# Moving the loads of the next head group from GpSimd to ScalarE, a quarter behind each block's exponentials

## The chip, the cores and the metric

The kernel runs on one core of one Trainium2 chip. The metric is device microseconds of one execution. Most executions of a kernel agree within 0.3%. In the profile, PE is TensorE's matmuls, PEld its weight loads, DVE is VectorE, ACT is ScalarE, POOL is GpSimd and SP is SyncE; a trailing q (ACTq, SPq, POOLq) marks an engine's instruction stream, where it issues transfers. PEclk is the TensorE clock that the throttle granted, 1.00 being full speed. An execution's time is about 2.0 us more than the span of its trace (941.21 against 939.2 us for the profiled execution of the kernel before).

## The reference, cut to what matters

```python
# x: [1, 2048, 640] bf16; 32 query heads, 32 kv heads, head size 192; only the last W = 512 keys count
xn = layernorm(x)
q  = (xn @ wq) -> 32 heads                    # wq: 640 x 6144
k, v = k_cache[:, :, Sk-512:, :], v_cache[:, :, Sk-512:, :]
s  = softmax(q k^T / sqrt(192)) v @ wo        # wo: 6144 x 640
g  = silu((sigmoid(xn w_gate) * (xn w_up)) @ w_down)
out = x + s * g
```

The part with w_gate, w_up and w_down is computed first (to about 165 us) and its gate is parked in device memory as `gB_d`. All that follows is attention, and the change is there.

## The kernel before

The 32 heads are worked in 8 groups of 2 pairs (`G = 2`, `NG = 8`), and each group in 4 blocks of 512 query rows (`NST = 4`): 32 blocks `(g, s)`. A group needs 12 loads of `wq`, 4 of `k`, 4 of `v` and 1 of `wo`. While group g is computed, `load_ahead(g + 1, s)` issues the loads of group g + 1 from GpSimd; it is called ahead of the block's matmuls, so the program's order lets GpSimd run as far ahead as buffers allow. SyncE issues the transposing transfers: `kT` (keys of the next group) and `oT` (each block's attention output, which the next block's `wo` matmuls read).

```python
def load_k(hp):                        # load_v, load_wq alike, all on nc.gpsimd
    k_sb = k_pool.tile([P, KC * PC, 2, HF], BF16, name="k_sb")      # k_pool has 2 buffers
    for i in range(2):
        nc.gpsimd.dma_start(k_sb[:, :, i, :], A_k_cache[...])       # cut

def turn_k(hp):
    kT = kt_pool.tile([P, KC * PC, P], BF16, name="kT")
    nc.sync.dma_start_transpose(kT[:], k_of[hp][:].rearrange("p k i e -> p (k i e)"))

def load_ahead(g, s):
    hps = range(g * G, (g + 1) * G)
    if s == 0:
        for hp in hps: load_k(hp)
    elif s == 1:
        for hp in hps:
            load_v(hp)
            turn_k(hp)
    elif s == 2:
        for hp in hps: load_wq(hp)
    if s == NST - 1:
        load_wo(g)

def stage_s(n, pp, c):                 # scores (L428), then the exponential (L432)
    ...
    nc.scalar.activation(E_t[n, pp][:, c, :, :], ps, AF.Exp, scale=scale_qk)

def stage_pv(n, pp, i):                # P V (L444), division, then, after the pair's second head:
    ...
        oT = oT_pool.tile([P, TQ * PC, P], BF16, name="oT")
        nc.sync.dma_start_transpose(oT[:], o_st[:].rearrange("p q d -> p (q d)"))   # L457

load_wo(0)
for u in range(G * PC // 2): stage_q(0, u)
for n, (g, s) in enumerate(blocks):
    if g + 1 < NG:
        load_ahead(g + 1, s)
    for k, (pp, c) in enumerate(todo):            # 8 score steps and exponentials
        stage_s(n, pp, c)
        if ...: stage_q(n + 1, k // 2)            # q of the next block (L412)
    for k, u in enumerate(pv):                    # 4 steps
        stage_pv(*u)
        if wo: stage_wo(*wo[k])                   # wo of the block BEFORE this one (L489): reads oT
```

Two more users of GpSimd: `load_gate` and `prep_load` fetch tiles of the gate and of x (128 rows of 640, 32 and 16 of them) for the last two groups, and in the last blocks GpSimd does the final addition of an output tile (L500).

The softmax here doesn't subtract the row's maximum and nothing guards it: scores larger than these inputs give would overflow.

## Time and profile before

| | kernel before |
|---|---|
| time, median of 3 runs | 937.3 us (936.82 to 939.11) |
| time of the execution that was profiled | 941.21 us (span 939.2) |
| TensorE busy | 923.3 us, 98% |
| period of an attention block, steady | 23.83 us |
| block 1 of 32 in the profiled execution | 27.96 us |
| loads issued by GpSimd | 232 |

From the page of the kernel before: the span; busy time, share and number of instructions of each engine; the queue of GpSimd's transfers (packets, MB, share of 16 engines' span); the shares of the chain that ended last; and the transfers of `wq` (count, KB each, median us from issue to landing).

```profile
span 939.2 us, 18233 instructions
...
PE 923.3 (98%) x7945; PEld 541.1 (58%) x8025; DVE 446.9 (48%) x636; ACT 303.8 (32%) x340; POOL 222.4 (24%) x277
...
q0 software_dynamic: 13440, 38.81, 19.5%
...
PE 95%; DMA 2%; issue 1%; POOL 1%; DVE 1%; ACT 0%; SPq 0%; DVEq 0%; ACTq 0%
...
wqp<-in_A_wq_dram POOLq DMA_DIRECT2D x96, 80.0 KB, 4.9
...
```

TensorE is the limit: 98% busy, and 95% of the chain. GpSimd's 222.4 us are mostly the issuing of transfers, and hardly any of them lie on the chain (POOL 1%). What is unusual is the 2% of the chain that lies on a DMA, `oT<-o_st`. The list of what TensorE waited for (total us, times, longest us) has it as one single wait; the one below it belongs to the start of the program:

```profile
...
PE ps_all L489 <- DMA oT<-o_st: 2.3, 1, 2.3
PE ps_all L248 <- DVE warm L243: 1.5, 1, 1.5
...
```

The timeline of TensorE in the same execution (start us, length us, what; in brackets the idle time before it and what ended it) places it in block 1, whose score matmuls start at 188.32 us:

```profile
...
201.45 0.98 PE L489 MATMUL ps_all<-wo_g,oT 128*128 128x512 bf16 x5
204.75 1.15 PE L489 MATMUL ps_all<-wo_g,oT 128*128 128x512 bf16 x6 [2.33 <-DMA oT<-o_st]
205.70 2.79 PE L444 MATMUL ps_all<-v_sb_99,E 128*128 128x193 bf16 x16
208.28 2.08 PE L489 MATMUL ps_all<-wo_g,oT 128*128 128x512 bf16 x12
210.20 1.52 PE L444 MATMUL ps_all<-v_sb_101,E 128*128 128x193 bf16 x16
...
```

After the 2.33 us stop, 16 matmuls of L444 take 2.79 us where they take 1.52 us elsewhere. The view by stretch (stretch, its length, busy us of each engine, granted clock, DMA share, GB/s) says why:

```profile
...
188.30:201.40 13.10, 13.10 (x125) 6.50 (x125) 4.82 (x6) 7.67 (x8) 2.12 (x3) 1.00 1.15 149
201.40:205.00 3.60, 1.22 (x10) 0.58 (x9) 1.14 (x2) 0.08 (x1) 0.00 (x0) 1.00 1.37 114
205.00:209.00 4.00, 4.00 (x25) 3.19 (x24) 1.20 (x3) 0.00 (x0) 2.04 (x2) 0.57 1.28 148
...
```

In the third stretch the clock granted was 0.57; a narrower stretch, 205.45 to 208.86 us, has 0.50, and the clock was full on both sides of it. Stop and slow clock together make block 1 last 27.96 us, 4.13 us over the period (2.33 us of stop and half of the 3.41 us at half clock are 4.04 us of it). The cause visible before it is a burst: by GpSimd's timeline, the `wo` of group 0 and then the whole of group 1 (22 loads) are issued between 169.74 and 190.4 us, and SyncE's stream meanwhile has the two transposes of block 0 and the two of the keys, of which the latter take 14.54 us to issue. Three lines of GpSimd's timeline, two lines of SyncE's, and the time that the 64 transfers `oT` took from issue to landing (shortest, median, longest):

```profile
...
170.57 4.06 POOL L123 DMA_DIRECT2D k_sb<-in_A_k_cache_dram  x4
...
186.03 3.57 POOL L151 DMA_DIRECT2D wqp<-in_A_wq_dram  x5 [0.54 <-DMA v_sb_111<-in_A_v_cache_dram]
189.59 0.84 POOL L379 DMA_DIRECT2D wo_g<-in_A_wo_dram  x1
...
186.95 4.02 SPq L457 DMA_TRANSPOSE oT<-o_st  x2
191.06 14.54 SPq L158 DMA_TRANSPOSE kT<-k_sb  x2
...
DMA to landing us min/median/max: 3.6/3.9/15.0
```

### The profile page before, as it was taken

The page shows a single profiled execution, that of the slowest core. Times are in us where ns is not written, and L with a number is a line of the kernel's source. Part 1 is how long each engine was busy: PE and PEld are TensorE (multiplying, and loading weights), DVE is VectorE, ACT ScalarE, POOL GpSimd, SP SyncE. Part 2 cuts the span into 40 slices and gives each one's busy share as a digit, 9 for nine tenths or more (in the row PEclk, how much of TensorE's full clock was granted, in tenths as well). Part 3 has the DMA queues.
Part 4 walks back from the last instruction along what each step waited for, and adds up shares of the span by engine and source line. Part 5 has one row for each costly group of instructions (what it writes and reads, how often), then busy time and mean ns, then how long its engine had stood idle before and what let it go on. Part 6 is the DMA issues. An engine that isn't in the chain of part 4 may idle for free.

```text
span 939.2 us, 18233 instructions
## 1 busy us (share of the span) xinstructions
PE 923.3 (98%) x7945; PEld 541.1 (58%) x8025; DVE 446.9 (48%) x636; ACT 303.8 (32%) x340; POOL 222.4 (24%) x277
## 2 busy tenths in 40 slices
PE   9999999989999999999999999999999999999996
PEld 5545445555555565555556556555566665665664
DVE  5453522434444444444444444444444444444655
ACT  4333322433333333333333333333333333333340
POOL 0060000620042004200410041004010207966005
PEclk9999999999999999999999999999999999999999
DMA  9566130692257225622664175326632543553434
GB/s 290 144 124 119 21 92 15 151 143 50 44 102 140 38 43 102 137 41 37 109 118 61 35 110 111 68 34 110 110 69 35 96 68 84 128 144 89 99 84 118
DMA packets 160383, 87.18 MB, mean 93 GB/s; under 512 B 139184, under 2 KB 151600, under 8 KB 160304
## 3 DMA queue, kind: packets, MB, share of 16 engines
q1 hardware_dynamic: 146864, 47.20, 27.2%
q0 software_dynamic: 13440, 38.81, 19.5%
q8 instruction: 63, 1.03, 0.5%
q14 instruction: 16, 0.13, 0.0%
HBM read 44.70 MB, written 5.24 MB: 53 GB/s over the span
## 4 chain that ended last, share of the span: by engine, by line
PE 95%; DMA 2%; issue 1%; POOL 1%; DVE 1%; ACT 0%; SPq 0%; DVEq 0%; ACTq 0%
PE ps_all L412 21%; PE ps_all L489 21%; PE ps_all L444 19%; PE ps_all L428 17%; PE ps_all L319 10%; PE ps_all L339 6%; DMA oT<-o_st 2%; PE ps_all L260 1%; POOL o_sb L500 1%; DMA x_sb_138<-in_A_x_dram 0%; ACT E L432 0%; DVE t_sb L499 0%; POOL gBa_sb L462 0%; DVE o_st L451 0%; DVE stats L222 0%
## 5 line engine op out<-in xcount | busy, mean ns | idle before, releaser
L432 ACT ACTIVATE E<-ps_all 128x1024 bf16<-128x1024 f32 x256 | 247.8, 1022 | 500.4 <-PE ps_all L428 453.4
L489 PE MATMUL ps_all<-wo_g,oT 128*128 128x128 bf16 (+2 forms) x1473 | 225.6, 296 | 5.6 <-DMA oT<-o_st 2.3
L417 DVE CAST qT<-ps_all 128x1024 bf16<-128x1024 f32 x96 | 117.6, 1225 | 226.3 <-PE ps_all L412 226.3
L428 PE MATMUL ps_all<-qT,kT 64*128 64x512 bf16 x1536 | 186.7, 376 | 0.0
L444 PEld LDWEIGHTS <-E 128*128 128x128 bf16 x2048 | 172.0, 98 | 24.6 <-issue 13.3
L489 PEld LDWEIGHTS <-oT 128*128 128x128 bf16 x1536 | 121.6, 98 | 78.9 <-DMA oT<-o_st 2.7
L412 PEld LDWEIGHTS <-wqp 64*128 64x128 bf16 x1920 | 93.4, 94 | 113.8 <-issue 0.3
L428 PEld LDWEIGHTS <-kT 64*128 64x128 bf16 x1536 | 72.3, 94 | 91.8 <-issue 8.4
L451 DVE TENSOR_TENSOR o_st<-ps_all,rden 128x768 bf16<-128x768 f32 x128 | 122.6, 958 | 4.9 <-DVE rden L450 0.5
L151 POOL DMA_DIRECT2D wqp<-in_A_wq_dram x96 | 68.8, 727 | 12.0 <-DMA wqp<-in_A_wq_dram 8.6
L450 DVE RECIPROCAL rden<-ps_all 128x4 f32<-128x4 f32 x128 | 23.4, 182 | 100.1 <-PE ps_all L444 99.9
L325 DVE TENSOR_TENSOR hT_sb<-ps_all,sig_sb 128x512 bf16<-128x512 f32 x48 | 33.1, 692 | 51.0 <-PE ps_all L319 41.2
L412 PE MATMUL ps_all<-xnT_95,wqp 64*128 64x512 bf16 x240 | 55.7, 376 | 0.0
L412 PE MATMUL ps_all<-xnT_96,wqp 64*128 64x512 bf16 x240 | 55.7, 376 | 0.0
L412 PE MATMUL ps_all<-xnT_94,wqp 64*128 64x512 bf16 x240 | 55.7, 376 | 0.0
L412 PE MATMUL ps_all<-xnS_91,wqp 64*128 64x512 bf16 x240 | 55.6, 376 | 0.0
L412 PE MATMUL ps_all<-xnS_92,wqp 64*128 64x512 bf16 x240 | 55.6, 376 | 0.0
L412 PE MATMUL ps_all<-xnS_90,wqp 64*128 64x512 bf16 x240 | 55.6, 376 | 0.0
L412 PE MATMUL ps_all<-xnT_93,wqp 64*128 64x512 bf16 x240 | 55.4, 376 | 0.0
L412 PE MATMUL ps_all<-xnS_89,wqp 64*128 64x512 bf16 x240 | 55.3, 376 | 0.0
L339 PE MATMUL ps_all<-wd_sb,hT_sb 128*128 128x128 bf16 (+1 forms) x377 | 52.4, 298 | 0.4
L123 POOL DMA_DIRECT2D k_sb<-in_A_k_cache_dram x32 | 32.5, 1021 | 68.2 <-DMA kT<-k_sb 68.2
(163 smaller groups left out, 742.7 us busy)
## 6 DMA issues: line engine op xcount, KB each, us to landing
wqp<-in_A_wq_dram POOLq DMA_DIRECT2D x96, 80.0 KB, 4.9
wo_g<-in_A_wo_dram POOLq DMA_DIRECT2D x8, 960.0 KB, 8.3
k_sb<-in_A_k_cache_dram POOLq DMA_DIRECT2D x32, 192.0 KB, 4.7
gBa_sb<-gB_d POOLq DMA_DIRECT2D x32, 160.0 KB, 2.7
gB_d<-gB_sb POOLq DMA_DIRECT2D x16, 160.0 KB, 2.5
xa_sb<-in_A_x_dram POOLq DMA_DIRECT2D x16, 160.0 KB, 3.2
out_dram<-o_sb SPq DMA_DIRECT2D x15, 160.0 KB, 2.3
wd_sb<-in_B_w_down_dram SPq DMA_DIRECT2D x1, 1920.0 KB, 11.8
```

Source lines behind the costliest of these rows:

```text
L123: nc.gpsimd.dma_start(k_sb[:, :, i, :], A_k_cache[0, hk, Sk - W:Sk, :].rearrange("(p k) (j e) -> p (k j) e", k=KC, j=PC),)
L151: nc.gpsimd.dma_start(wqp[r, jj // 2, :, i, :], wq_r[:, :, :, d0:d0 + HF].rearrange("p c h n -> p (c h) n"),)
L319: nc.tensor.matmul(gu[:, i, :], lhsT=w[:, c, f * P:(f + 1) * P], rhs=xnT[s][:, c, :], start=(c == 0), stop=(c == NCD - 1),)
L325: nc.vector.tensor_tensor(hT_sb[:, f, :], gu[:, 1, :], sig_sb[:], ALU.mult)
L339: nc.tensor.matmul(oB_ps[:, d0:d0 + dsz], lhsT=hT_sb[:, f, q * P:(q + 1) * P], rhs=wd_sb[:, f, d0:d0 + dsz], start=(f == 0), stop=(f == NF ...
L412: nc.tensor.matmul(ps[:, b, :], lhsT=wq_t[g][r, u, 2 * c + h].rearrange("p i e -> p (i e)"), rhs=x[s][r, c, :], start=(c == 0 and h == 0), ...
L417: nc.vector.tensor_copy(qT_t[n][:, 2 * u:2 * u + 2, :], ps)
L428: nc.tensor.matmul(ps[:, b, :], lhsT=kT[r, c * PC + j, :], rhs=qT[r, pp * PC + j, :], start=(j == 0), stop=(j == PC - 1),)
L432: nc.scalar.activation(E_t[n, pp][:, c, :, :], ps, AF.Exp, scale=scale_qk)
L444: nc.tensor.matmul(o_ps[:, q // 2, q % 2, 0:DH + 1], lhsT=E[:, c, i, q * P:(q + 1) * P], rhs=vt[:, c, 0:DH + 1], start=(c == 0), stop=(c = ...
L451: nc.vector.tensor_tensor(o_st[:, :, i * DH:(i + 1) * DH].rearrange("p (b i) d -> p b i d", b=2), o_ps[:, :, :, 0:DH], rden[:].to_broadcas ...
L489: nc.tensor.matmul(oA[:, d0 - base:d0 - base + dsz], lhsT=oT_t[n, pp][:, q * PC + j, :], rhs=wo_t[g][:, cc, d0:d0 + dsz], start=(cc == 0), ...
```

## The change

The intent is to spread the loads of the next group over its four blocks and to take their issue from GpSimd to ScalarE, placed right behind the block's eighth exponential, where ScalarE would idle for 11.6 us. Block 0 of a group issues the first pair's 6 `wq` and 2 `k` loads, block 1 the second pair's, block 2 the 4 `v` loads and the key transposes, block 3 `wo`. The loads of group 0 stay on GpSimd. The diff, cut to its core:

```diff
-    def load_k(hp):
+    def load_k(hp, eng):                      # likewise load_v, load_wq, load_wo
...
-            nc.gpsimd.dma_start(
+            eng.dma_start(
...
     def load_ahead(g, s):
-        hps = range(g * G, (g + 1) * G)
-        if s == 0:
-            for hp in hps:
-                load_k(hp)
-        elif s == 1:
-            for hp in hps:
-                load_v(hp)
+        if s < G:
+            load_wq(g * G + s, nc.scalar)
+            load_k(g * G + s, nc.scalar)
+        elif s == G:
+            for hp in range(g * G, (g + 1) * G):
+                load_v(hp, nc.scalar)
                 turn_k(hp)
-        elif s == 2:
-            for hp in hps:
-                load_wq(hp)
         if s == NST - 1:
-            load_wo(g)
+            load_wo(g, nc.scalar)
...
     for n, (g, s) in enumerate(blocks):
-        if g + 1 < NG:
-            load_ahead(g + 1, s)
         todo = [(pp, c) for pp in range(G) for c in range(KC)]
         for k, (pp, c) in enumerate(todo):
             stage_s(n, pp, c)
             ...
+        if g + 1 < NG:
+            load_ahead(g + 1, s)
```

More of the change, by code (lines that the diff above doesn't have):

```diff
@@ L51 @@
     assert F % P == 0 and D % P == 0
-    assert HQ % 4 == 0
+    assert HQ % 4 == 0 and NST > 2
     NPAIR = HQ // 2
@@ L127, in load_k, with load_v @@
         k_of[hp] = k_sb
-    def load_v(hp):
+    def load_v(hp, eng):
         v_t[hp] = []
@@ L133, in load_v @@
             vt = v_tiles[(2 * hp + i) % NV]
-            nc.gpsimd.dma_start(
+            eng.dma_start(
                 vt[:, :, 0:DH],
@@ L138, in load_v, with load_wq @@
             v_t[hp].append(vt)
-    def load_wq(hp):
+    def load_wq(hp, eng):
         if hp % G == 0:
@@ L150, in load_wq @@
                 d0 = (2 * hp + i) * DH + j * HF
-                nc.gpsimd.dma_start(
+                eng.dma_start(
                     wqp[r, jj // 2, :, i, :],
@@ L353 @@
                 for hp in range(G):
-                    load_k(hp)
+                    load_k(hp, nc.gpsimd)
                 for hp in range(G):
-                    load_v(hp)
-                    load_wq(hp)
+                    load_v(hp, nc.gpsimd)
+                    load_wq(hp, nc.gpsimd)
             elif s == 1:
@@ L375, with load_wo @@
     wo_t = {}
-    def load_wo(g):
+    def load_wo(g, eng):
         wo_g = wo_pool.tile([P, G * PC, D], BF16, name="wo_g")
-        nc.gpsimd.dma_start(wo_g[:], wo_r[:, g * G * PC:(g + 1) * G * PC, :])
+        eng.dma_start(wo_g[:], wo_r[:, g * G * PC:(g + 1) * G * PC, :])
         wo_t[g] = wo_g
     def load_ahead(g, s):
-        hps = range(g * G, (g + 1) * G)
-        if s == 0:
-            for hp in hps:
-                load_k(hp)
-        elif s == 1:
-            for hp in hps:
-                load_v(hp)
+        if s < G:
[4 more added lines that the diff above has]
+                load_v(hp, nc.scalar)
                 turn_k(hp)
-        elif s == 2:
-            for hp in hps:
-                load_wq(hp)
         if s == NST - 1:
-            load_wo(g)
+            load_wo(g, nc.scalar)
     def stage_q(n, u):
@@ L534 @@
     qT_t, E_t, oT_t, ost_t = {}, {}, {}, {}
-    load_wo(0)
+    load_wo(0, nc.gpsimd)
     for u in range(G * PC // 2):
```

## The prediction

> **What bounds the kernel now.** TensorE. The page gives PE 923.3 of 939.2 us busy (98%); the chain of waits is 95% PE. From the third attention block on, blocks start every 23.83 us (217.75, 241.58, 265.41, 289.24 in the chain), with 23.73 us of PE work each (busy time by stretch), equally where GpSimd issues 7 to 11 loads and where it issues none. So in steady state no load of the next group is waited for; GpSimd waits for TensorE (46 us before a V load), not the reverse. The list of waits shows one PE wait for a DMA: 2.3 us on oT, at 202.4 us.
>
> That wait is what this change can win. At 170 to 190 us GpSimd issues wo and the whole of group 1 at once (k, v, 12 wq, wo). The transposes oT of block 0, issued at 187 and 188.4 us, then need up to 15.0 us to land (median 3.9). TensorE stops 2.33 us, and the granted clock of the following 4 us is 0.57, so 16 matmuls of L444 take 2.79 us instead of 1.52. Block 1 runs from 188.32 to 216.28: 27.96 us, 4.13 over the period. The Trainium skill, "TensorE: Matmul & The Clock Gate", section on the HAM clock gate, says that an idle window brings the half clock; this trace agrees (0.57).
>
> **What the change moves.** Per group 12 wq, 4 k, 4 v and 1 wo loads leave GpSimd (0.73, 1.02, 0.75, 0.84 us each; it is not critical, so this wins nothing) for ScalarE, behind the eighth exponential of a block: 8 loads in blocks 0 and 1 of a group, 4 in block 2, 1 in block 3. In block 0 only one pair's wq and k then compete with oT.
>
> **New cost, on ScalarE.** SyncE's first plain loads take 0.40 to 0.54 us to issue. Estimate: 6 x 0.45 + 2 x 0.8 = about 4.3 us for 8 loads; if the queue fills (6912 runs of 128 B; transposes of 1536 runs already hold SyncE up to 13 us), perhaps 6 to 11 us. ScalarE idles 11.6 us after the last exponential of a block (gaps before E), and TensorE, with four PSUM pairs, can take the next block's first exponential about 2.3 us later than now (estimate from the stage durations). So some 13.9 us are free: steady state should not change. Block 0 has no wo work and a gap of 5.1 us only, so a small stall at block 1 is possible. [...]
>
> **Sum.** 937.3 - 4.1 if the oT stall and its slow clock vanish wholly; 0.5 to 1 us less gain for a partial stall at block 1. Predicted 934.0 us, range 931.8 to 938.5. Faster by over 2%: 0.01; within 2%: 0.92; slower by over 2%: 0.07.
>
> **What would show it.** Right: the PE wait on oT is below 0.5 us and oT of block 0 lands in under 12 us; block 1 takes about 23.8 us; later blocks stay 23.83; GpSimd busy falls by some 100 us. Wrong: PE waiting for ACT at the start of blocks 1 and 2 of each group, period above 23.83 there.
>
> **What would make it wrong.** Loads of 128-byte runs on the hardware queue far slower than 30 ns each per engine, holding ScalarE beyond 14 us in the 14 blocks with 8 loads: each us over costs 14 us in all. Or the transposes, sharing the engines with many short packets, still land late in block 1, and the stall stays.

## The result, and the profile after

| | before | after |
|---|---|---|
| median of the runs taken together, 4 each | 937.37 us (936.82 to 939.11) | 938.0 us (937.91 to 938.1) |
| the execution profiled: time, span | 941.21, 939.2 us | 938.1, 936.1 us |
| block 1 in it | 27.96 us | 23.83 us |
| from the last matmul to the end of the span | 7.58 us | 8.38 us |

The ratio of after to before is 1.0004 (95% interval 0.9986 to 1.0021): the same. Ratios here are the mean time of one kernel's fast runs over the mean of the other's of the same rounds, so not quite the ratio of the medians that are quoted. The value lies inside the predicted range and 4 us above the predicted point.

The lines of the page after that answer to those above:

```profile
span 936.1 us, 18189 instructions
...
PE 921.1 (98%) x7945; PEld 539.8 (58%) x8025; DVE 446.7 (48%) x636; ACT 303.8 (32%) x340; POOL 106.8 (11%) x130
...
q10 hardware_dynamic: 118832, 24.78, 13.9%
q0 software_dynamic: 4368, 14.03, 5.7%
...
PE 96%; issue 1%; POOL 1%; DMA 0%; DVE 0%; ACT 0%; SPq 0%; DVEq 0%; ACTq 0%; POOLq 0%
...
wqp<-in_A_wq_dram ACTq DMA_DIRECT2D x84, 80.0 KB, 3.0
...
```

24.78 MB left GpSimd's queue q0 for a new hardware queue, q10; GpSimd's busy time halved; `wq` loads land in 3.0 us instead of 4.9; the share of DMA in the chain falls from 2% to 0%, and the slowest `oT` lands in 6.2 us instead of 15.0. TensorE's waits in the trace after have no `oT` line (the last line below is of the `oT` transfers again):

```profile
...
PE ps_all L248 <- DVE warm L243: 1.5, 1, 1.5
PE ps_all L260 <- DMA wu_sb<-in_B_w_up_dram: 0.4, 1, 0.4
PE ps_all L260 <- ACT xnT_93 L275: 0.3, 1, 0.3
...
DMA to landing us min/median/max: 3.6/3.8/6.2
```

In the stretches where the kernel before had stopped, TensorE now works through, at full clock:

```profile
...
188.30:201.40 13.10, 13.10 (x126) 6.35 (x124) 5.08 (x6) 7.42 (x8) 0.00 (x0) 1.00 0.74 97
201.40:205.00 3.60, 3.55 (x36) 2.77 (x35) 2.00 (x4) 0.33 (x1) 0.00 (x0) 1.00 0.63 100
205.00:209.00 4.00, 3.95 (x37) 2.82 (x37) 3.01 (x5) 0.00 (x0) 0.00 (x0) 1.00 0.83 123
...
```

ScalarE's timeline after shows one quarter of 8 loads in steady state. Loads and exponentials overlap in the list: the exponential of 366.60 us ends at 367.62, and the first load is issued at 367.25. The eight take from 367.25 to 373.85 us, and the next exponential still waits its 11.58 us for TensorE, exactly as in the kernel before:

```profile
...
366.60 1.02 ACT L429 ACTIVATE E<-ps_all 128x1024 bf16<-128x1024 f32 x1 [1.47 <-PE ps_all L425]
367.25 0.63 ACTq L151 DMA_DIRECT2D wqp<-in_A_wq_dram  x1
367.52 1.02 ACT L429 ACTIVATE E<-ps_all 128x1024 bf16<-128x1024 f32 x1
367.92 4.28 ACTq L151 DMA_DIRECT2D wqp<-in_A_wq_dram  x5
372.24 1.61 ACTq L123 DMA_DIRECT2D k_sb<-in_A_k_cache_dram  x2
380.12 1.94 ACT L429 ACTIVATE E<-ps_all 128x1024 bf16<-128x1024 f32 x2 [11.58 <-PE ps_all L425]
...
```

So the trace after does what was predicted, step by step, and the two profiled executions differ by 3.07 us: 4.13 us won in block 1, 0.25 us lost because attention starts later (171.27 against 171.02 us), and 0.80 us lost between the last matmul and the end. Yet the medians say that nothing was won. Either the profiled execution of before was not like the others, or something is taken back that the traces do not show.

### The profile page after: what moved, and what is told of

It is laid out like the page before. It is cut to its first block, busy times and chain, and to the rows that moved or that the text cites. A ratio compares the mean times of both kernels' runs of the same rounds, so it can differ in the third digit from the quotient of the medians.

```text
span 936.1 us, 18189 instructions
## 1 busy us (share of the span) xinstructions
PE 921.1 (98%) x7945; PEld 539.8 (58%) x8025; DVE 446.7 (48%) x636; ACT 303.8 (32%) x340; POOL 106.8 (11%) x130
## 3 DMA queue, kind: packets, MB, share of 16 engines
q1 hardware_dynamic: 146864, 47.20, 25.8%
q10 hardware_dynamic: 118832, 24.78, 13.9%
## 4 chain that ended last, share of the span: by engine, by line
PE 96%; issue 1%; POOL 1%; DMA 0%; DVE 0%; ACT 0%; SPq 0%; DVEq 0%; ACTq 0%; POOLq 0%
PE ps_all L409 22%; PE ps_all L486 21%; PE ps_all L441 19%; PE ps_all L425 18%; PE ps_all L319 10%; PE ps_all L339 6%; PE ps_all L260 1%; DMA x_sb_138<-in_A_x_dram 0%; POOL o_sb L497 0%; ACT E L429 0%; DVE t_sb L496 0%; POOL gBa_sb L459 0%; DVE stats L222 0%; SPq L175 0%; ACT xnT_93 L275 0%
## 5 line engine op out<-in xcount | busy, mean ns | idle before, releaser
L324 ACT ACTIVATE sig_sb<-ps_all 128x512 bf16<-128x512 f32 x48 | 28.6, 597 | 56.6 <-PE ps_all L319 56.2
```

The lines of the kernel that those rows point to most:

```text
L324: nc.scalar.activation(sig_sb[:], gu[:, 0, :], AF.Sigmoid)
```

## The experiments

All kernels gave correct results, and the record marks all runs as fast (none is over 1.5% above the fastest of its kernel). At the limit of 2%, only e4 differs from the kernel before; the smaller differences below rest on the intervals and on the spread of the runs. The kernel before was timed again in each of the four batches, on three chips (the first two on one), with medians of 937.28 us (e1 to e4, 11 runs), 937.86 (e5 to e8, 11 runs, four of them above 938.5), 937.37 (e9 to e11, 11 runs) and 937.42 (e12, 13 runs). The texts give letters to the theories. In words, those that the account needs: the stall is a matter of chance and common executions of before don't have it (A), or it is in all of them and the change loses as much elsewhere (B); the small copies that pace a variant shorten the program's end (C), or the number or the order of GpSimd's loads sets it (D); the last GpSimd transfers lie too near the end (E); each GpSimd load of 128 rows has its fixed share in the last drain (F); the key transposes in front of `oT` cause the stall (S1), or the burst of loads alone does (S2).

### 1. The two kernels again

No edit: the kernel before (e1) and the kernel after (e2), 5 rounds each.

> The kernel before, unchanged, profiled and timed again. Theory A (chance): the 4.13 us of block 1 seen in the profile of before (whose own time was 941.21 us against a median of 937.4 us) is in only some executions. Then most timed runs lie at 936.8 to 937.5 us, a few at 939 to 941, and a profile that falls on a common run shows no PE wait on oT, block 1 of 23.8 us and a span near 935.2 us. Theory B (paid back): the stall is in every execution of before, and the changed kernel loses the same 3.5 us elsewhere. Then this profile shows the wait on oT of 2 us or more again, block 1 of about 28 us and a span near 939 us.

> The changed kernel, unchanged, on the same chip. Theory A: 938.0 us within 0.2, in every run, 0.5 to 1.0 us above the common run of before, because the end of the program (from the last vector instruction to the end of the span) takes 5.2 us here against 4.4 us in before. Theory B: the same time, but no constant difference at the end of the program: the loss lies in the attention blocks, whose period would exceed 23.83 us somewhere.

Before: median 937.28 us, with five of six runs between 937.11 and 937.36 and one at 941.94. Its profile fell on a common run (937.28 us), and there is no wait on `oT`: the blocks from block 1 on all take 23.83 us, and the slowest `oT` of the whole execution lands in 8.8 us. The first two of the stretches, in this execution of the same kernel, and its `oT` transfers:

```profile
...
188.30:201.40 13.10, 13.10 (x126) 6.36 (x124) 5.02 (x6) 7.47 (x8) 2.42 (x4) 1.00 1.11 219
201.40:205.00 3.60, 3.60 (x36) 2.77 (x35) 2.05 (x4) 0.28 (x1) 3.60 (x4) 1.00 0.53 114
...
DMA to landing us min/median/max: 3.6/3.8/8.8
```

And SyncE's stream there issues the key transposes in 8.29 us instead of 14.54:

```profile
...
187.15 4.03 SPq L457 DMA_TRANSPOSE oT<-o_st  x2
191.28 8.29 SPq L158 DMA_TRANSPOSE kT<-k_sb  x2
...
```

In the stretch before the stop the DMA engines were as busy (shares 1.11 and 1.15), but moved 219 GB/s in the common run and 149 GB/s in the stalled one. The first profile of before was of a run that is not typical, and its own time, 941.21 us against a median of 937.3, had said so.

After: median 937.85 us, 937.71 to 938.05 in six runs. Against e1's profile the whole difference of the spans can be laid out: 936.11 − 935.23 = 0.88 us, of which 0.05 us is a later start of attention, 0 is in the blocks, and 0.83 us lies between the last matmul and the end (8.39 or 8.38 us in each trace of after, 7.55 us in e1).

All executions of the kernel before, 57 of them over all batches, give the share of the odd ones: 15 are above 938.5 us, from 938.83 to 945.66; the other 42 have a mean of 937.32. Nine of the 15 are as long as the first profile's 941.21 us or longer. The runs above 941 us have a granted clock of 0.995 to 0.997, the common ones 0.997 to 0.999, as a stop with a slow clock after it would have it. But of the 15 only the first profile left a trace, so that the other 14 are stalls on `oT` is inferred, not shown. The mean of all 57 is 938.46 us and the mean of the ten runs of after is 937.92: against the common runs the change loses 0.6 us, and in the mean it seems to win 0.5 us, but with a standard error of 0.3 us from the spread of the runs that gain is not clear of noise.

### 2. Pacing without ScalarE

e3 keeps the order and the quarters of the kernel after, but GpSimd issues them. What holds GpSimd back is a copy of one column that reads the block's last exponential:

```diff
+    pace = small.tile([P, 1], BF16, name="pace")
-    def load_ahead(g, s):
+    def load_ahead(n, g, s):
+        nc.gpsimd.tensor_copy(pace[:], E_t[n, G - 1][:, KC - 1, 1, 0:1])
         if s < G:
-            load_wq(g * G + s, nc.scalar)         # likewise k, v, wo
+            load_wq(g * G + s, nc.gpsimd)
```

> The quarters of the changed kernel, in the same order, but issued by GpSimd, held back by one tiny GpSimd copy that reads the block's last exponentials. If it is the pacing that removes the stall of block 1 and not the engine that issues: no PE wait on oT, block 1 of 23.8 us, 936.8 to 937.6 us in every run (no stall, and the end of the program as in before, 4.4 us). If the engine matters (GpSimd's transfers delay the transposes however they are paced): oT of block 0 still takes over 12 us to land and the wait of about 2 us appears in the profile, 939 to 941 us in some runs.

935.27 us (935.02 to 935.45), ratio 0.9970 (0.9946 to 0.9995). GpSimd's timeline in e3 shows what the pacing does (a copy, then a quarter, then nothing until the next block's exponentials are done):

```profile
...
184.40 0.19 POOL L385 COPY pace<-E 128x1 bf16<-128x1 bf16 x1 [13.66 <-ACT E L432]
184.52 4.28 POOL L151 DMA_DIRECT2D wqp<-in_A_wq_dram  x6
188.79 2.04 POOL L123 DMA_DIRECT2D k_sb<-in_A_k_cache_dram  x2
201.78 0.19 POOL L385 COPY pace<-E 128x1 bf16<-128x1 bf16 x1 [10.95 <-ACT E L432]
202.25 4.40 POOL L151 DMA_DIRECT2D wqp<-in_A_wq_dram  x6 [0.28 <-issue]
...
```

There is no `oT` wait, all blocks from block 1 on take 23.83 us, and the run-to-run spread is 0.4 us. So the stall goes by the pacing; ScalarE is not needed for it. The Trainium skill, "DMA: Bandwidth & Descriptors", section "Issuing engines are not separate DMA queues", says that transfers issued by different engines run on the same 16 DMA engines and interleave there, and that issuing elsewhere saves only the issuing engine's time, "usually small relative to the DMA itself". A `wq` load takes 0.66 us to issue from ScalarE and 0.73 us from GpSimd, and where both are paced alike it lands in 3.0 us (after) or 2.9 us (e3), so the 4.9 us of before belong to its burst and not to the engine. The 2.0 us that e3 gains on the median of before, where no stall is to be removed, were not expected: the trace has them at the end. From the last matmul to the end of the span e3 takes 5.73 us, before 7.55 (section 4).

### 3. The same loads in the middle of the exponentials

e4 is the kernel after with the quarter issued after the block's second exponential:

```diff
-        if g + 1 < NG:
-            load_ahead(g + 1, s)
+            if k == 1 and g + 1 < NG:
+                load_ahead(g + 1, s)
```

> The changed kernel with each quarter issued by ScalarE between the second and third exponential of its block instead of behind the eighth. Tests the estimate of the free time: 8 loads hold ScalarE about 6 us, which from there puts the third and fourth exponential 1.2 to 1.5 us past the point where TensorE needs their PSUM pair; 14 blocks times 1.5 us = about 21 us slower, 956 to 962 us, period of those blocks about 25.3 us, and the blocks with 4 or 1 loads unchanged at 23.83. If issuing costs ScalarE nothing that matters wherever it stands, it stays at 938 us.

968.06 us (964.27 to 969.24), ratio 1.0307 (1.0266 to 1.0347): more than expected. TensorE waits for exponentials, once in each of the 14 blocks that issue 8 loads:

```profile
...
PE ps_all L425 <- ACT E L429: 22.7, 14, 3.8
...
```

ScalarE's timeline in one of them:

```profile
...
394.19 1.02 ACT L429 ACTIVATE E<-ps_all 128x1024 bf16<-128x1024 f32 x1
394.55 4.14 ACTq L151 DMA_DIRECT2D wqp<-in_A_wq_dram  x5
398.73 1.76 ACTq L123 DMA_DIRECT2D k_sb<-in_A_k_cache_dram  x2
400.60 3.77 ACT L429 ACTIVATE E<-ps_all 128x1024 bf16<-128x1024 f32 x4 [5.39 <-DMA wqp<-in_A_wq_dram]
...
```

The third exponential comes at 400.60 us, 5.39 us after the second; blocks with 8 loads take 25.0 to 27.6 us (block 0 takes 22.94 instead of 17.3), blocks with 4 or 1 take 23.83. Against the kernel after the loss is 30.2 us; the waits are 22.7 us of it. TensorE's busy time is also 6.9 us longer (932.5 us on e4's page, 925.6 on e2's); about half of that are two stretches at half clock, of 3.4 us each, behind two of the waits, and the rest was not taken apart. The issue of eight loads costs ScalarE the same 6 us in both kernels. What makes it free in the kernel after is the place: behind the eighth exponential ScalarE has nothing to do for 11.58 us.

### 4. What makes the end of the program longer?

In the trace's instruction records GpSimd's stream closes with a DRAIN, which the page does not count as busy. In before and after the end of this drain comes later than that of any other engine's, 0.78 us before the end of the span (only short ones, of 0.1 us at most, follow it), and the time from GpSimd's last addition to the end of the drain is 4.91 us before and 5.73 us after, in every trace of the two. Five kernels take that apart.

e5 adds only the 28 copies of e3 to the kernel after (the first three added lines of e3's diff, the loads staying on ScalarE).

> The changed kernel (loads on ScalarE) plus only the 28 tiny GpSimd copies of e3, one per block that loads. In e3 the last drain of GpSimd ended 2.7 us after its last addition, in before 4.9 us, in the changed kernel 5.7 us, with the same additions. Theory C: the copies shorten that drain. Then here too it ends about 2.7 us after the last addition and the time is 935.0 to 935.5 us. Theory D: the drain depends on who issues the group loads (their number on GpSimd or their order). Then the copies change nothing: 5.7 us, 937.8 to 938.1 us.

937.63 us (937.44 to 938.24), ratio 0.9981 (0.9946 to 1.0016), drain 5.73 us. Copies do nothing to it.

e6 is the kernel after with the 5 gate tiles of the last two blocks fetched by ScalarE, so that GpSimd has no load in its last 36 us:

```diff
-    def load_gate(t):
+    def load_gate(t, eng=nc.gpsimd):
         gB_sb = gate_pool.tile([P, D], BF16, name="gBa_sb")
-        nc.gpsimd.dma_start(gB_sb[:], gB_d[t * P:(t + 1) * P, :])
+        eng.dma_start(gB_sb[:], gB_d[t * P:(t + 1) * P, :])
...
-                    gates[tt] = load_gate(tt)
+                    gates[tt] = load_gate(tt, nc.scalar if n >= last - 1 else nc.gpsimd)
```

> The changed kernel with the last 5 loads of gB, issued during the final block, on ScalarE instead of GpSimd (0.55 us each between GpSimd's last additions). If only the issue time counts: the last addition ends about 1.3 us earlier, the drain stays 5.7 us, 936.4 to 936.9 us. Theory E: GpSimd's last drain waits for work that GpSimd's own late DMA issues leave behind. Then it falls below 2 us as well and the end of the program is set by SyncE's last output instead: 933.5 to 935 us.

936.39 us (936.09 to 936.82), ratio 0.9968 (0.9940 to 0.9996). The drain still takes 5.32 us: it does not wait for a late transfer. It is 0.41 us shorter for 5 loads fewer, 0.082 us a load; most of the rest of the gain is that four of the five issues no longer stand between GpSimd's last additions: the last one ends 0.90 us after the last matmul instead of 1.88.

e7 is e3 with e6's edit.

> e3 (quarters paced on GpSimd) with the last 5 loads of gB on ScalarE. If only the issue time counts: 1.0 to 1.5 us less than e3's 935.27, so 933.8 to 934.3 us, the best so far. Under theory E the drain is shorter too, but SyncE's last output then ends the program, and the time is the same 933.5 to 934.3 us; so the drain itself tells E apart here, not the time.

934.62 us (934.32 to 935.08), ratio 0.9948 (0.9917 to 0.9979), a little above the range expected (933.8 to 934.3). The drain is 2.30 us, again 0.41 us below that of e3.

e10 is e3 without the copies: GpSimd issues in the order of the kernel after, as early as buffers allow.

> e3 without its pacing copies: the order of the quarters and of the k transposes as in the changed kernel, issued by GpSimd as early as it gets to them. Tells order from pacing. Stall: under S1 none (k transposes are late); under S2 (burst) runs above 938.5 us come back. End of the program: if the order of GpSimd's loads sets the last drain, 2.7 us after the last addition as in e3, common run 935.3 us; if the pacing in time sets it, 4.9 us as in before, common run 937.3 us.

935.86 us, ratio 0.9982 (0.9963 to 1.0001), but in two kinds: four runs of 935.56 to 935.90 and two of 937.24 and 937.40. The drain is 2.71 us, as in e3, so it is the order of GpSimd's loads and not their pace that the drain follows (the later key transposes, which e10 has too, don't do it: e9 below has them alone, and 4.91 us). Without the pace the stall comes back; the profile, of a run of 935.90 us, has a small one (a single wait of 0.4 us on `oT`, block 1 at 24.51 us, the slowest `oT` at 14.6 us).

e11 takes all 48 tile loads of 128 rows away from GpSimd in the kernel after (the five of e6 to ScalarE, the other gate tiles and those of x to SyncE), which leaves GpSimd 37 transfers, the last of them issued at 169 us:

```diff
-    def load_gate(t):
+    def load_gate(t, eng=nc.sync):
...
-        nc.gpsimd.dma_start(x_sb[:], xf[t * P:(t + 1) * P, :])
+        nc.sync.dma_start(x_sb[:], xf[t * P:(t + 1) * P, :])
...
-                    gates[tt] = load_gate(tt)
+                    gates[tt] = load_gate(tt, nc.scalar if n >= last - 1 else nc.sync)
```

> e6 with all other loads of gB and x of the attention part (43 of them, 128 rows each) moved from GpSimd to SyncE as well; GpSimd then issues 37 DMAs in all. Taking 5 such loads from GpSimd shortened the last drain by 0.41 us in two pairs (changed kernel to e6: 5.73 to 5.32; e3 to e7: 2.71 to 2.30), 0.082 us each. Theory F: the drain works off something left by GpSimd's own DMA issues, in proportion. Then 5.32 - 43 x 0.082 = 1.8 us, SyncE's last output ends the program, and the time is 934.0 to 934.6 us. If the proportion is chance: drain 4 us or more, 936.0 to 936.9 us. Danger: SyncE's transposes wait behind these loads; a wait on oT would show it.

934.53 us (934.06 to 934.84), ratio 0.9963 (0.9945 to 0.9981). The drain takes 1.81 us, where 0.082 us a load had given 5.73 − 48 × 0.082 = 1.8. SyncE's closing drain is now the last, as it was already in e3, e7 and e10 (in e3 by 0.4 us): from there on a shorter drain of GpSimd no longer shortens the program by itself. The table collects the ends, from the instruction records of the profiled executions:

| kernel | GpSimd transfers | last addition to end of drain | last matmul to end | median us |
|---|---|---|---|---|
| before (e1) | 232 | 4.91 | 7.55 | 937.28 |
| after (e2) | 85 | 5.73 | 8.39 | 937.85 |
| e5, after + copies | 85 | 5.73 | 8.39 | 937.63 |
| e6, after, 5 gate tiles from ScalarE | 80 | 5.32 | 7.00 | 936.39 |
| e11, after, no tile loads on GpSimd | 37 | 1.81 | 5.06 | 934.53 |
| e3, paced on GpSimd | 232 | 2.71 | 5.73 | 935.27 |
| e10, e3's order, unpaced | 232 | 2.71 | 5.73 | 935.86 |
| e7, e3 with 5 gate tiles from ScalarE | 227 | 2.30 | 5.30 | 934.62 |
| e9, before, key transposes a block later | 232 | 4.91 | 7.56 | 937.33 |
| e12, e9 with no tile loads on GpSimd | 184 | 1.57 | 4.77 | 935.39 |

The number of transfers alone does not decide: 232 of them give 4.91 us in one order and 2.71 us in another. Within one order, each tile load of 128 rows counts 0.082 us, in two orders (e6 and e11 against after, e7 against e3). e12, described below, breaks the line: 4.91 − 48 × 0.082 is 1.0, and it measured 1.57, so 0.070 us a load. What the drain does in that time is not in the trace, and stays open, and so does why it grew by 0.82 us when the group loads left GpSimd.

### 5. What makes oT late?

e8 gives the kernel before one copy, ahead of block 1's loads. It holds back, once, the `v`, `wq` and `wo` loads of group 1 until block 0's exponentials are done: the burst is not thinned, only shifted by some 10 us.

```diff
+    pace = small.tile([P, 1], BF16, name="pace")
     for n, (g, s) in enumerate(blocks):
+        if n == 1:
+            nc.gpsimd.tensor_copy(pace[:], E_t[0, G - 1][:, KC - 1, 1, 0:1])
         if g + 1 < NG:
             load_ahead(g + 1, s)
```

> The kernel before with one single tiny GpSimd copy, which reads the last exponentials of block 0 and stands after the k loads of group 1, so v, wq and wo of group 1 wait for it. Pacing of the first group alone: no wait on oT in the profile and no run above 938.5 us (of the kernel before, 5 of 22 runs so far were above). Theory C with a single copy enough: the last drain ends about 2.7 us after the last addition, 935.0 to 935.5 us; if it needs more copies, or C is wrong: 4.9 us and 936.8 to 937.5 us.

This was a miss, and an instructive one: 945.67 us (945.2 to 948.1), ratio 1.0072 (1.0039 to 1.0104), in every one of its five runs. The burst (184 to 201 us) now lies upon the transposes, the slowest `oT` lands in 21.5 us, and TensorE stops twice:

```profile
...
PE ps_all L489 <- DMA oT<-o_st: 5.8, 2, 3.2
...
```

Block 2, which reads the `oT` of block 1, takes 32.23 us, 8.4 over the period. So with the same loads, it matters where in time they fall: shifted by 10 us, the stall comes in every run instead of now and then.

e9 asks whether the two key transposes, which SyncE issues between the `oT` of block 0 and that of block 1, are the part of the traffic that does it: it moves them a block later in the kernel before.

```diff
         elif s == 1:
             for hp in hps:
                 load_v(hp)
-                turn_k(hp)
         elif s == 2:
             for hp in hps:
                 load_wq(hp)
+                turn_k(hp)
```

> The kernel before with one part of the change alone: the transposes of k move from block 1 to block 2 of a group; loads stay on GpSimd, unpaced. Of the kernel before, 9 of 33 runs were above 938.5 us, up to 945.3. Theory S1: the stall needs the k transposes right behind those of block 0, so that four transposes and the burst of loads are in flight together. Then it is gone: no run of this kernel above 938.5, no wait on oT. Theory S2: the burst of loads alone delays oT. Then slow runs remain, about one in four, or the stall moves to another block. The end of the program as in before (drain 4.9 us after the last addition) if it depends on the loads' order, and the common run at 937.3 us.

937.33 us (936.84 to 937.61), ratio 0.9994 (0.9974 to 1.0014), no stalled run in six, no wait on `oT`. With about one stalled run in four for the kernel before, six common runs in a row happen by chance in 0.74 to the power 6, some 16% of cases, so this proves little.

e12 is e9 with e11's edit (no tile loads on GpSimd).

> e9 (the kernel before with the k transposes one block later, group loads on GpSimd, unpaced) and, as in e11, all 48 loads of gB and x of the attention part off GpSimd (5 on ScalarE in the final block, 43 on SyncE). A test of both conclusions on another base. Theory F, 0.082 us of the last drain per load taken away: 4.91 - 48 x 0.082 = 1.0 us, SyncE's last output ends the program, 934.0 to 934.7 us as e11, though the group loads never moved to ScalarE. If the drain is a property of the order and not proportional, it can be anything from 0 to 6 us, and above 3 us the time is 935 us or more. S1: no run above its median by 1 us, no wait on oT; S2: some runs 2 to 8 us longer, as in the kernel before.

Three runs of 934.40 to 934.70 us and three of 936.09, 936.44 and 939.71, median 935.39, ratio 0.9981 (0.9964 to 0.9999). Its profile, a run of 936.44 us, has the stall in block 1 (25.82 us), with the `oT` landing in up to 14.5 us:

```profile
...
PE ps_all L489 <- DMA oT<-o_st: 1.8, 1, 1.8
...
```

```profile
...
187.29 28.30 SPq L457 DMA_TRANSPOSE oT<-o_st  x4
215.70 3.74 SPq L158 DMA_TRANSPOSE kT<-k_sb  x2
```

SyncE had issued nothing but the four `oT` by then; the key transposes came at 215.70 us. So S1 falls: the stall comes without them, with the burst of GpSimd's loads alone in front of it. The edit that differs from e9 does not act at that time, since the first tile loads that it moves come in the last two groups. Why, under the same burst, a transpose lands in 9 us in one execution and in 15 in the next, was not found.

Over all kernels whose loads are paced (after with e2, e3, e5, e6, e7 and e11: 38 runs; e4, whose TensorE waits for ScalarE, left aside) no run is more than 0.7 us above its kernel's median; if one in four stalled, 38 in a row without a stall would be a chance of about 1 in 100,000. Of those unpaced, the kernel before has 15 odd runs in 57, e10 two in 6, e12 three in 6, e9 none in 6, and all of e8's are stalled. The cleanest pair is e3 and e10: the same order and the same engine, with the pace (0 of 6) and without it (2 of 6).

## Why the prediction was right or wrong

**"What bounds the kernel now. TensorE" and "in steady state no load of the next group is waited for".** Right. The blocks take 23.83 us before and after, and taking 147 loads from GpSimd (232 to 85) won nothing as such.

**"That wait is what this change can win."** Right for the execution that was read, wrong for the kernel. The wait on `oT`, the slow clock behind it and the 4.13 us were read correctly, the cause was named correctly (e3 against e10 shows that the pace removes the stall, e12 that it needs no key transposes), and the change does remove them. But one execution in four is above 938.5 us (15 of 57), and only 9 of 57 are as long as that one.

**"Sum. 937.3 - 4.1".** This is the step that failed. The 4.1 us were measured in an execution of 941.21 us and were subtracted from the median of other executions, which do not contain them. The sum with matching terms is 941.21 − 4.13 = 937.1 us, within 0.9 us of what was measured. The time of the profiled execution stood beside the median from the start; a gap of 3.9 us where runs agree within 0.3% was the warning.

**"0.5 to 1 us less gain for a partial stall at block 1", "a small stall at block 1 is possible".** It did not come. ScalarE's first quarter makes one exponential wait 5.3 us in block 1, but TensorE does not wait for it: blocks 1 and 2 take 23.83 us.

**"about 4.3 us for 8 loads; if the queue fills [...] perhaps 6 to 11 us", against "some 13.9 us [...] free".** The mechanism was right, and so was the conclusion: eight loads took about 6.3 us (from 0.63 + 4.28 + 1.61 = 6.5 us in the quarter shown to 0.73 + 3.44 + 2.12 = 6.3 us in the first one), the low end of the upper guess, and the free time covered it. e4 shows the price where it does not: 22.7 us of waits.

**"far slower than 30 ns each per engine".** It did not come either. (The page before gives SyncE's queue 146864 packets and 27.2% of 16 engines' span, 27.8 ns each.) The page after gives ScalarE's queue 118832 packets 13.9% of 16 engines' span: 0.139 × 16 × 936.1 us / 118832 = 17.5 ns each.

**What was missing.** The end. The prediction has no term for GpSimd's last drain, which became 0.82 us longer and makes the common runs of after 0.6 us slower than those of before. With the two terms, no stall to remove in the median and +0.8 us at the end, the sum, made afterwards, is 937.3 + 0.8 = 938.1 us against 938.0 measured.

**The range and the class.** Right, but by luck as far as the range goes: what the prediction had in mind for a slower result was a cost on ScalarE or a stall that stays, and neither came. The value landed there for two other reasons, a median that held no stall and a longer end.

## What to carry to other kernels

Before subtracting a stall that a trace shows, compare the time of the profiled execution with the median of the others: when it lies above by the size of the stall, the stall may be a matter of chance, and a second profile can tell (e1). Removing such a stall narrows the spread, as here, but has nothing to take from the median. Prefetches that may run far ahead gather into bursts that collide with transfers on the critical path; a pace tied to the block's own work removed that here on both issuing engines that were tried, and ScalarE's issue is free only where ScalarE would idle anyway. Look at the end of the program as well: here moving 48 small loads off GpSimd (e11: 934.53 us) or pacing the loads on GpSimd in the new order with five of the small ones moved (e7: 934.62 us) both beat the kernel before by about 3 us, 0.3%, and the kernel after by more.

## What the Trainium skill lacked or had wrong

- "TensorE: Matmul & The Clock Gate", Part 1 (the HAM clock gate), gives the half clock as the default and as what follows at least one idle window of about 3.4 us. The traces agree in kind, but not in the length: in before a stop of 2.33 us was followed by half clock (0.50 from 205.45 to 208.86 us), and in e4 one of 1.95 us by 3.41 us of it, while the clock stayed at 1.00 after stops of 1.82 us (e12), 2.20 us and 2.26 us (both e4). A stop shorter than the window can be enough, and its length alone does not decide.
- "VectorE: DVE Perf Modes", section "The DRAIN you can't avoid", knows the drains of a program's opening and closing as constant ones of about 12 ns on all engines, and "Perfetto Trace Analysis", section "Sequencer-only Instruction (DRAIN, etc)", only says which part of one is recorded. SyncE's closing drains of 0.01 us fit that. GpSimd's closing drain took 3.14 to 7.80 us here and ended 1.57 to 5.73 us after its last addition, in a way that repeats from trace to trace of a kernel and depends on which transfers GpSimd had issued, and in which order: 0.082 us for each tile load of 128 rows within one order (e6, e7, e11; 0.070 in e12), 4.91 against 2.71 us for the same 232 transfers in two orders. No page has this.
- No page that was read has the spread of a transposing transfer's landing under load: the slowest `oT` of the kernel before landed in 8.8 us in one execution and 15.0 us in another of the same program, and in 21.5 us with the burst upon it; the median is 3.9 us.
